# ScalarE makes the low bits of every piece of the first weight, instead of every second piece

## The chip, the cores and the metric

The kernel runs on one core of a Trainium2 chip. The metric is device time in microseconds (us) for one execution. The core has TensorE (PE, matrix multiplies; its weight loads are listed as PEld), VectorE (DVE), ScalarE (ACT), GpSimd (POOL) and SyncE (SP), which here only issues DMAs. Each engine works through its own instructions in the order in which they were written out.

## The reference, cut to what matters

Two parts follow each other: a landmark (Nystrom) attention over q, k and v of shape 8 x 8 x 576 x 64, and, on its output x of 8 x 576 x 512, a Fourier mixing, a normalisation and a two-layer MLP with weights of 512 x 2048 and 2048 x 512.

```python
A, Bm, C = sm(q, k_lm), sm(q_lm, k_lm), sm(q_lm, k)      # 32 landmarks: means of 18 rows
Z = Bm.T / (norm1(Bm) * norminf(Bm) + 1e-06)
for _ in range(6):
    Z = 2 * Z - Z @ Bm @ Z                               # Newton steps to the inverse
x = (A @ Z @ C @ v)                                      # then heads side by side
u = x + real(fft2(x))
un = (u - mean(u)) / sqrt(var(u) + 1e-06)
out = u + relu(un @ w_ch1) @ w_ch2
```

Both weights come as float64. q, k and v are float32.

## The kernel before, in words

One generator per job (`attention`, `weights`, `mlp`) gives out instructions. A planner in `run` keeps a clock of its own (`now`) from rough costs, and resumes the first of them that is due: attention has priority 1, weights 2, the MLP 3. So each instruction's place follows from what the planner thinks that the earlier ones cost. TensorE's order is written out exactly as the planner gave it. While nothing is due, and the MLP's second layer has not begun, the planner puts filler matmuls (`acc<-idle,ones`, 128x256) on TensorE, whose result nobody reads. On the other engines, a scheduler places the instructions by the same order, with extra order edges that the class `Timed` adds. All VectorE, ScalarE and GpSimd instructions go through `Timed` (line L138 in the profile), all matmuls through `mm` (L243), transposes through `tr` (L252), the fillers that are asked for by number through `warm` (L247).

The part around the change is `weights`. A weight is 16 pieces of 128 x 512 numbers, each piece a DMA of 512 KB of raw float64 words. There are 32 pieces: 0 to 15 of the first weight, 16 to 31 of the second. Each goes through:

1. `prepare`: one ScalarE Prelu of the words' upper halves makes sign and magnitude (`row<-w`, or `row<-big` where the raw words lie in a `big` buffer). It runs up to four pieces ahead.
2. The three low bits that float32 still takes from the words' lower halves. For even pieces VectorE shifts the lower half right by 29 (TENSOR_SCALAR `w<-w` 128x512 int32). For odd pieces ScalarE scales the top byte of the lower half and rounds it (ACTIVATE `w<-w` 128x512 int32 from uint8).
3. The joining: VectorE ors the shifted magnitude and the low bits (SCALAR_TENSOR_TENSOR `w<-row,w`). I call it the decode of the piece.
4. `squares`: four small matmuls of the piece on itself (`acc<-w` 128x128) that add up to a Gram matrix, two pieces behind the decode. Ahead of the last of a weight stand 24 fillers.
5. After the last piece of a weight, `scale` takes the diagonal (`wd`, `wm`), sums it by a matmul (`h<-wm,ones` for the first weight), takes a power on GpSimd (`wp_r<-wp_e`) and writes the weight's scale `wsc`.
6. `halve`: the split of a piece into a high and a low float16 half, ScalarE for the high (`w<-w,wsc`), VectorE for the low (SCALAR_TENSOR_TENSOR `w<-w,wsc`). The first weight's splits begin once its scale is known, two with each decode of the second weight (`PACE = 2`). The high half of piece i is written over the float32 room of piece i-2, so ScalarE's split of i waits until VectorE's split of i-2 has read it.

Beside it runs batch 0 of the attention: row sums of k and q, scores, softmax, six Newton steps (`RE`, `E`), a transform of the folded scores (`big<-at` after the matmuls `at<-t,mid` and `at<-t1t,row`), the product with v (`R`), its bound (`wm`), the factors `Wt` and `Wx`, their transform (`mid<-at` 128x262), and then in `mix` and `norm`: row tiles `u`, their statistics (`bn`), the normalised rows (TENSOR_SCALAR `row<-u,mv,r`, "the normalised tiles" below), their transposes on TensorE (`at<-ident,row`) and the split of those into `unT`.

The MLP works on two row tiles at a time (a chunk). A pair of the first weight's split pieces gives one `h` (24 matmuls `h<-unT,w` of 128x256), which ScalarE (Relu, the high half) and VectorE (the low half) evict. `h` has two PSUM buffers. Eight `h` make up a chunk. The second layer (`acc<-w,h` or `acc<-w,mid` 128x512) begins once the second weight has its scale and its first splits.

Of the kernel before, what the change touches and what calls it, by code (L numbers as in the profile page):

```python
# [20 lines left out]
NF = DF // P  # L21
# [12 lines left out]
AHEAD, PREP, EARLY = 1, 4, 2  # L34
# [124 lines left out]
class Kernel:  # L159
# [119 lines left out]
    def weights(self):  # L279
        nc = self.nc  # L280
        V, A = self.V, self.A
        whole = self.whole
        slots = [[t[:, OFF + 512 * i : OFF + 512 * i + 512] for i in range(NF)] for t in whole]
        upper = [[t.bitcast(BF16).rearrange("p (m x) -> p m x", x=2)[:, :, 1] for t in ss] for ss in slots]
        hl = [[t[:, 512 * i : 512 * i + 512].bitcast(F16).rearrange("p (y m) -> p y m", y=2) for i in range(NF)] for t in whole]
        self.w1s = [t.rearrange("p y (c f) -> p y c f", c=KT) for t in hl[0]]
        self.w2s = hl[1]
        sc = self.cp.tile([P, 3], F32, name="wsc")
        pieces = [(w, f) for w in range(2) for f in range(NF)]
        mags = []  # L290

        def prepare(i):


            mag = self.row(512)
            top = self.wraw[i].rearrange("p (m x) -> p m x", x=2)[:, :, 1].bitcast(F32)
            A.late = self.raw_there[i] if i < 2 * NF - PREP else 0.0
            A.activation(mag, top, AF.Prelu, scale=2.0**-112, alpha=-(2.0**32))
            mags.append(mag)

        def squares(i):

            w, f = pieces[i]
            if i == NF - 1:
                self.warm(24)
            for c in range(KT):
                x = upper[w][f][:, P * c : P * c + P]
                self.mm(self.gram[:, P * w : P * w + P], x, x, i == 0 and c == 0, f == NF - 1 and c == KT - 1)

        es = []  # L310

        def scale(w):

            dg, a2 = self.small(P, "wd"), self.small(1, "wm2")
            V.tensor_tensor(dg, self.gram[:, P * w : P * w + P], self.ident, ALU.mult)
            V.tensor_reduce(a2, dg, AX.X, ALU.add)
            if w:
                self.sum(1, 0, 2)
            yield self.till(a2, banks=1) if w else max(0.0, self.there[a2.name] - self.now)
            ps = self.psum() if w else self.ps_h.tile([P, 512], F32, name="h")  # L320
            self.mm(ps[:, 0:1], self.ones, a2)
            if w == 0:
                self.warm(8)
            self.scaled = True
            e, r = self.small(1, f"wp{w}_e"), self.small(1, f"wp{w}_r")
            V.tensor_scalar(e, ps[:, 0:1], 2.0**-120, 2.0**126, ALU.max, ALU.min)
            self.G.tensor_tensor(r, e, self.mhalf[:, 0:1], ALU.pow)
            if w:
                self.sum(1, 0, 3)
            V.tensor_scalar(r.bitcast(I32), r.bitcast(I32), 0x7F800000, None, ALU.bitwise_and)  # L330
            V.reciprocal(e, r)
            es.append(e)
            V.tensor_scalar(sc[:, w : w + 1], r, (2.0**12, 2.0**14)[w], None, ALU.mult)

        def halve():
            w, f = pieces[sum(self.split_w)]
            self.split(hl[w][f][:, 0], hl[w][f][:, 1], slots[w][f], sc[:, w : w + 1])
            self.split_w[w] = f + 1

        for i, (w, f) in enumerate(pieces):  # L340
            while len(mags) < min(2 * NF, i + 1 + PREP):
                j = len(mags)
                while len(self.wraw) < min(2 * NF, j + 1 + AHEAD):
                    self.raw()
                if self.raw_there[j] > self.now:
                    if j > i:
                        break
                    yield self.raw_there[j] - self.now
                    continue
                prepare(j)  # L350
            low = self.wraw[i].rearrange("p (m x) -> p m x", x=2)[:, :, 0]
            x, dst = mags[i].bitcast(I32), slots[w][f].bitcast(I32)
            (A if i % 2 else V).late = self.raw_there[i] if i < 2 * NF - PREP else 0.0
            if i % 2 == 0:
                V.tensor_scalar(dst, low, 29, None, ALU.logical_shift_right)
            else:
                byte = self.wraw[i].bitcast(mybir.dt.uint8).rearrange("p (m x) -> p m x", x=8)[:, :, 3]
                A.activation(dst, byte, AF.Copy, scale=2.0**-5, bias=-0.484375)
            V.scalar_tensor_tensor(dst, x, 3, dst, ALU.logical_shift_left, ALU.bitwise_or)
            if i > 1 and not NF <= i < NF + 2:  # L360
                squares(i - 2)
            self.decoded = i + 1
            if self.decoded == 2 * NF:
                self.load(1)
            yield max(0.0, max(self.V.free, self.G.free) - self.now - WT)
            if i == NF - 1:
                squares(NF - 2)
                yield 0.0
                squares(NF - 1)
                yield from scale(0)  # L370
            for _ in range(PACE if es else 0):
                if self.split_w[0] < NF:
                    halve()
                    yield max(0.0, max(self.V.free, self.G.free) - self.now - WT)
        squares(2 * NF - 2)
        self.lm1 = self.sums(None)
        self.sum(1, 0, 0)
        yield 0.0
        squares(2 * NF - 1)
        self.sum(1, 0, 1)  # L380
        self.magnitude(1, 0)
        yield from scale(1)
        V.tensor_scalar(sc[:, 2:3], es[0], 2.0**-25, es[1], ALU.mult, ALU.mult)
        self.inv2 = sc[:, 2:3]
        while sum(self.split_w) < 2 * NF:
            halve()
            yield max(0.0, max(self.V.free, self.A.free) - self.now - WT)
# [55 lines left out]
    def sum(self, b, e, i):  # L443

        loads, lm = (self.loads[1], self.lm1[0]) if b == 1 and e == 0 else (self.live, self.lm)
        V = self.V
        V.late = self.now if b == 2 else 0.0
        x, o = divmod(i, 2)
        if x == 0:
            part, kf = lm[:, 1, e, 32 * o : 32 * o + 32], loads[e][0][:, S * o : S * o + S]  # L450
            first = V.tensor_reduce(part, kf.rearrange("p (m t) -> p m t", t=18), AX.X, ALU.add)
        else:
            lv = lm[:, 0, e].rearrange("p (x o m) -> p x o m", o=2, m=8)
            qv = loads[e][1][:, 0 : 16 * SEG].rearrange("p (x o t) -> p x o t", o=2, t=2 * SEG)
            first = V.tensor_reduce(lv[:, :, o], qv[:, :, o, o : o + 144].rearrange("p x (m t) -> p x m t", t=18), AX.X, ALU.add)
        if b == 1:
            self.tc.keep_in_program_order(first)
# [664 lines left out]
```

## Time and profile before

| | before |
|---|---|
| median of 3 runs | 991.0 us (988.72 to 992.71) |
| profiled execution, its own time | 990.97 us |
| its span, first to last instruction | 989.2 us |
| what lies around the span | 1.8 us |
| PE busy | 959.0 us (97%), fillers included |
| DVE busy | 594.0 us (60%) |
| ACT busy | 319.7 us (32%) |
| mean granted TensorE clock | 0.989 of 2.4 GHz |

Busy times are sums over the whole span. A row's duration runs over into the next instruction of the same engine: two VectorE instructions of 0.68 us take 1.28 us, not 1.36, and three ScalarE instructions of 0.68 us take 1.83 us. So the text takes 0.60 us for such a VectorE instruction in a queue, and 0.57 to 0.60 us for a ScalarE one.

### The profile page before, as it was taken

To read this page: it belongs to the slowest core of one execution; us is meant where nothing else is said; L and a number is where in the kernel's file an instruction comes from. 1 tells how busy PE (TensorE), PEld (TensorE's weight loads), DVE (VectorE), ACT (ScalarE), POOL (GpSimd) and SP (SyncE) were. 2 spreads that over 40 slices of the span, in tenths; PEclk is the share of its full clock that TensorE was granted. 3 is DMA by queue.
4 is the path that set the end of the run, shared out by engine and by line. 5 is a ranking of instruction groups with operands and counts; after the bars stand their busy time and mean duration, and the time that the engine had idled before them with its cause. 6 is when DMAs were issued, how large, how long until landed. Compare 5 with 4: busy or idle time off the path is not lost.

```text
span 989.2 us, 20815 instructions
## 1 busy us (share of the span) xinstructions
PE 959.0 (97%) x8726; PEld 666.7 (67%) x8726; DVE 594.0 (60%) x1609; ACT 319.7 (32%) x652; POOL 120.6 (12%) x124
## 2 busy tenths in 40 slices
PE   7878999999999999999999999999999999999998
PEld 5667756667666776677666776676666767666665
DVE  7889896895567735486467736784634835141111
ACT  5468743242224322143214322332213422020110
POOL 0000000022021301123011301150110401010000
PEclk7799999999999999999999999999999999999999
DMA  9844304235021511026112421145121301020000
GB/s 331 280 186 154 103 13 161 38 64 176 22 44 42 154 50 22 28 52 164 36 44 38 110 99 43 23 62 172 22 34 33 51 3 42 22 34 23 1 22 22
DMA packets 97774, 74.66 MB, mean 75 GB/s; under 512 B 68112, under 2 KB 86544, under 8 KB 97552
## 3 DMA queue, kind: packets, MB, share of 16 engines
q1 hardware_dynamic: 97680, 73.34, 26.8%
q8 instruction: 68, 1.11, 0.5%
q14 instruction: 26, 0.21, 0.1%
HBM read 48.02 MB, written 9.44 MB: 58 GB/s over the span
## 4 chain that ended last, share of the span: by engine, by line
PE 70%; DVE 1%; DMA 0%; ACT 0%; issue 0%; DVEq 0%
PE acc L243 30%; PE h L243 30%; PE at L243 10%; DMA out_dram<-u 0%; DVE u L138 0%; DVE h L138 0%; ACT h L138 0%; DVE w L138 0%; DVE row L138 0%; DVEq L138 0%
## 5 line engine op out<-in xcount | busy, mean ns | idle before, releaser
L243 PE MATMUL h<-unT,w 128*128 128x256 f16 x3456 | 408.4, 273 | 3.6 <-DVE w L138 2.9
L243 PEld LDWEIGHTS <-w 128*128 128x128 f16 (+1 forms) x3584 | 343.7, 98 | 76.8 <-DVE w L138 7.3
L243 PE MATMUL acc<-w,h 128*128 128x512 f16 x1632 | 380.9, 379 | 0.9 <-DVE w L138 0.9
L243 PEld LDWEIGHTS <-h 128*128 128x128 f16 x1632 | 157.2, 98 | 160.2 <-issue 3.7
L138 DVE SCALAR_TENSOR_TENSOR h<-h 128x512 f16<-128x512 f32 x136 | 93.6, 688 | 227.4 <-ACT h L138 227.3
L138 ACT ACTIVATE h<-h 128x512 f16<-128x512 f32 x136 | 81.1, 596 | 328.7 <-PE h L243 328.5
L138 POOL TENSOR_TENSOR r<-ve,mhalf 128x2 f32<-128x2 f32 (+1 forms) x20 | 13.7, 685 | 476.8 <-DVE ve L138 472.4
L138 POOL TENSOR_TENSOR mid<-mid 128x640 f16<-128x640 f32 (+2 forms) x36 | 49.6, 1388 | 165.6 <-ACT mid L138 128.8
L138 DVE TENSOR_REDUCE lm<-big 128x32 f32<-128x576 f32 x64 | 46.1, 742 | 3.0 <-DMA big<-k_dram 2.5
L243 PEld LDWEIGHTS <-big 128*128 128x128 f16 (+1 forms) x864 | 39.6, 102 | 8.0 <-issue 1.9
L243 PEld LDWEIGHTS <-mid 64*128 64x128 f16 (+1 forms) x624 | 30.2, 97 | 16.0 <-issue 9.5
L138 ACT CAST row<-row 128x512 f16<-128x512 f32 (+1 forms) x40 | 20.9, 554 | 61.7 <-DVE row L138 60.6
L138 POOL TENSOR_TENSOR row<-row 128x512 f16<-128x512 f32 (+1 forms) x33 | 35.4, 1088 | 38.0 <-ACT row L138 37.4
L138 DVE SCALAR_TENSOR_TENSOR u<-at,scw,w 128x128 f32<-128x128 f32 (+3 forms) x105 | 33.8, 389 | 7.2 <-PE at L243 5.2
L138 DVE SCALAR_TENSOR_TENSOR u<-acc,wsc,u 128x512 f32<-128x512 f32 x36 | 26.8, 748 | 11.1 <-PE acc L243 11.1
L243 PEld LDWEIGHTS at<-RE,E 128*128 128x128 f32 x192 | 26.9, 197 | 9.1 <-DVE RE L138 3.3
L243 PE MATMUL at<-RE,E 128*128 128x64 f32 (+1 forms) x192 | 29.4, 277 | 3.1 <-DVE RE L138 2.5
L138 DVE SCALAR_TENSOR_TENSOR w<-at,scw,w 128x262 f32<-128x262 f32 (+1 forms) x42 | 18.6, 486 | 22.5 <-ACT w L138 22.4
L138 DVE TENSOR_TENSOR E<-at,mask 128x256 f32<-128x256 f32 x48 | 20.1, 420 | 19.7 <-PE at L243 19.6
L243 PE MATMUL at<-mid,big 128*128 128x262 f16 (+1 forms) x288 | 31.2, 276 | 0.0
L138 DVE TENSOR_TENSOR mid<-mid 128x256 f32<-128x256 f32 (+2 forms) x52 | 30.8, 626 | 0.0
L138 DVE SCALAR_TENSOR_TENSOR big<-big,aq_r 128x1024 f16<-128x1024 f32 (+1 forms) x32 | 26.9, 870 | 3.5 <-ACT big L138 3.5
(184 smaller groups left out, 906.3 us busy)
## 6 DMA issues: line engine op xcount, KB each, us to landing
w<-w_dram SPq DMA_DIRECT2D x22, 512.0 KB, 6.7
big<-v_dram SPq DMA_DIRECT2D x16, 640.0 KB, 9.6
big<-q_dram SPq DMA_DIRECT2D x16, 584.0 KB, 5.9
big<-k_dram SPq DMA_DIRECT2D x16, 576.0 KB, 5.1
out_dram<-u SPq DMA_DIRECT2D x36, 256.0 KB, 2.0
big<-w_dram SPq DMA_DIRECT2D x10, 512.0 KB, 6.5
t<-t_dram SPq DMA_DIRECT2D x1, 1048.0 KB, 10.2
unT<-row SPq DMA_TRANSPOSE x64, 2.4
```

Source lines behind the costliest of these rows:

```text
L138: ins = call(out, *args, **kw)
L243: self.nc.tensor.matmul(out, a, b, start=start, stop=stop, skip_group_check=True)
```

## The change

For the first weight (`i < NF`, pieces 0 to 15) ScalarE makes the low bits of all pieces. For the second, even pieces stay with VectorE and odd ones with ScalarE.

```diff
             low = self.wraw[i].rearrange("p (m x) -> p m x", x=2)[:, :, 0]
             x, dst = mags[i].bitcast(I32), slots[w][f].bitcast(I32)
-            (A if i % 2 else V).late = self.raw_there[i] if i < 2 * NF - PREP else 0.0
-            if i % 2 == 0:
+            by_act = i % 2 or i < NF
+            (A if by_act else V).late = self.raw_there[i] if i < 2 * NF - PREP else 0.0
+            if not by_act:
                 V.tensor_scalar(dst, low, 29, None, ALU.logical_shift_right)
             else:
                 byte = self.wraw[i].bitcast(mybir.dt.uint8).rearrange("p (m x) -> p m x", x=8)[:, :, 3]
```

Eight VectorE instructions go and eight ScalarE instructions come. Because the planner's clock follows the cost of each engine, the places of many others change with them.

VectorE, where the first normalised tiles and their transposes stand. `wd`, `wm`, `wp_e`, `wp_r`, `wsc` are the steps of `scale`, `w_73<-w_73,wsc` a split of the first weight, `w_74<-row,w_74` a decode of the second, `row<-u,mv,r` the normalised tiles, `unT<-at,unT` the eviction of their transposes. Before:

```order
L138 TENSOR_TENSOR wd<-acc_109,ident 128x128
L138 TENSOR_TENSOR rt<-r_937 128x2
L138 TENSOR_REDUCE wm_1001<-wd 128x1
L138 SCALAR_TENSOR_TENSOR rt<-rt,ve 128x2
L138 SCALAR_TENSOR_TENSOR r_939<-rt,r_937 128x2
L138 TENSOR_SCALAR wp_e<-h 128x1
L138 TENSOR_SCALAR row<-u,mv,r_939 128x512 x2
L138 TENSOR_SCALAR wp_r<-wp_r 128x1
L138 RECIPROCAL wp_e<-wp_r 128x1
L138 TENSOR_SCALAR wsc<-wp_r 128x1
L138 SCALAR_TENSOR_TENSOR w_73<-w_73,wsc 128x512
L138 SCALAR_TENSOR_TENSOR unT<-at,unT 128x4x128 x2
```

The same place of the changed kernel:

```order
L138 TENSOR_TENSOR rt<-r_1013 128x2
L138 SCALAR_TENSOR_TENSOR w_74<-row,w_74 128x512
L138 SCALAR_TENSOR_TENSOR rt<-rt,ve 128x2
L138 SCALAR_TENSOR_TENSOR w_73<-w_73,wsc 128x512
L138 SCALAR_TENSOR_TENSOR r_1015<-rt,r_1013 128x2
L138 SCALAR_TENSOR_TENSOR w_74<-row,w_74 128x512
L138 TENSOR_SCALAR row<-u,mv,r_1015 128x512 x2
L138 SCALAR_TENSOR_TENSOR w_73<-w_73,wsc 128x512
L138 TENSOR_SCALAR w_74<-w_74 128x512
L138 SCALAR_TENSOR_TENSOR w_73<-w_73,wsc 128x512
L138 TENSOR_SCALAR w_74<-big 128x512
L138 SCALAR_TENSOR_TENSOR unT<-at,unT 128x4x128 x2
```

The steps of `scale` now stand far ahead of the normalised tiles; between `wsc` and `unT` there are eight splits, four decodes and three low-bit instructions of the second weight, where there was one split.

VectorE, a little earlier: where the scale is taken. `w_73<-row,w_73` is a decode of the first weight, `mid<-at,mid` the transform of `Wt`, `row<-at,scw,row` the first step of `mix`. Before, first, and then the changed kernel:

```order
L138 SCALAR_TENSOR_TENSOR mid<-at,mid 128x262 x4
L138 SCALAR_TENSOR_TENSOR w_73<-row,w_73 128x512
L138 TENSOR_SCALAR w_73<-w_74 128x512
L138 SCALAR_TENSOR_TENSOR w_73<-row,w_73 128x512
L138 SCALAR_TENSOR_TENSOR row<-at,scw,row 128x262 x2
L138 SCALAR_TENSOR_TENSOR w_73<-row,w_73 128x512
L138 TENSOR_SCALAR w_73<-w_74 128x512
L138 SCALAR_TENSOR_TENSOR u<-at,scw,row 128x256
```

```order
L138 SCALAR_TENSOR_TENSOR mid<-at,mid 128x262 x4
L138 SCALAR_TENSOR_TENSOR w_73<-row,w_73 128x512 x3
L138 TENSOR_TENSOR wd<-acc_109,ident 128x128
L138 TENSOR_REDUCE wm_915<-wd 128x1
L138 TENSOR_SCALAR w_74<-big 128x512
L138 TENSOR_SCALAR wp_e<-h 128x1
L138 TENSOR_SCALAR wp_r<-wp_r 128x1
L138 RECIPROCAL wp_e<-wp_r 128x1
L138 SCALAR_TENSOR_TENSOR row<-at,scw,row 128x262 x2
L138 TENSOR_SCALAR wsc<-wp_r 128x1
```

The last three decodes and the whole of `scale` moved ahead of `mix`; before they were spread through it.

TensorE, at the end of the Newton steps. `RE,E` 128x32 is the last step; `at<-t1t,row` ends a transform of the folded scores. Before, it stood behind the first of the two transforms; in the changed kernel it stands behind the second. First the rows before, then the changed ones:

```order
L243 MATMUL at<-t1t,row 128x320
L243 MATMUL at<-RE,E 128x32 x2
L243 LDWEIGHTS w_73
L243 MATMUL acc_109<-w_73 128x128
L243 LDWEIGHTS w_73
```

```order
L243 MATMUL at<-t1t,row 128x320
L243 LDWEIGHTS row
L243 MATMUL at<-t1t,row 128x320
L243 MATMUL at<-RE,E 128x32 x2
L243 LDWEIGHTS w_73
L243 MATMUL acc_109<-w_73 128x128
```

Between the second transform and the product `at<-R,Yd` there was nothing; now there are this last step, two pieces' squares and three fillers. The number of fillers in the whole program goes from 156 to 153.

## Rows read from the trace of the kernel before

**Rows 1.** The page: busy time of each engine, and the busy share in 40 equal slices of 24.7 us, in tenths (9 is 90% or more; PEclk is the granted clock in tenths).

```profile
PE 959.0 (97%) x8726; PEld 666.7 (67%) x8726; DVE 594.0 (60%) x1609; ACT 319.7 (32%) x652; POOL 120.6 (12%) x124
...
DVE  7889896895567735486467736784634835141111
ACT  5468743242224322143214322332213422020110
...
PEclk7799999999999999999999999999999999999999
```

**Rows 2.** Busy time of each engine by stretch: us from the span's start and length, then PE, PEld, DVE, ACT, POOL, the granted clock, the DMA share and GB/s.

```profile
0.00:71.00 71.00, 55.44 (x597) 42.50 (x598) 57.89 (x181) 37.18 (x79) 2.28 (x8) 0.86 0.80 277
71.00:86.00 15.00, 11.40 (x118) 8.80 (x117) 14.32 (x34) 13.58 (x28) 1.07 (x1) 1.00 0.30 105
86.00:116.00 30.00, 29.05 (x303) 25.54 (x301) 27.09 (x53) 22.27 (x40) 0.56 (x1) 1.00 0.51 159
...
400.00:980.00 580.00, 579.85 (x5087) 399.83 (x5085) 298.57 (x797) 149.24 (x304) 78.89 (x77) 1.00 0.20 49
```

**Rows 3.** What TensorE's matmuls waited for between 71 and 142 us: us in total, times, longest.

```profile
PE h L243 <- DVE w L138: 2.9, 4, 1.1
PE acc L243 <- DVE w L138: 1.3, 2, 0.9
PE h L243 <- DVE unT L138: 0.7, 1, 0.7
PE acc L243 <- ACT w L138: 0.5, 1, 0.5
```

**Rows 4.** Groups of VectorE and ScalarE instructions by form between 10 and 72 us: count, busy us, mean ns of one, idle time before. The first is the decode, the second the low bits on VectorE, the third the low bits on ScalarE.

```profile
L138 DVE SCALAR_TENSOR_TENSOR w<-row,w 128x512 int32<-128x512 int32 x16 | 10.9, 679 | 0.2
L138 DVE TENSOR_SCALAR w<-w 128x512 int32<-128x512 int32 x8 | 3.4, 420 | 0.0
L138 ACT ACTIVATE w<-w 128x512 int32<-128x512 uint8 x8 | 5.5, 685 | 0.0
```

**Rows 5.** The same between 71 and 89 us: VectorE's and ScalarE's splits.

```profile
L138 DVE SCALAR_TENSOR_TENSOR w<-w,wsc 128x512 f16<-128x512 f32 x9 | 6.7, 750 | 0.1
L138 ACT ACTIVATE w<-w,wsc 128x512 f16<-128x512 f32 x11 | 7.8, 718 | 0.7 <-DVE w L138 0.7
```

**Rows 6.** VectorE in order of time: start, duration (of all the instructions of the row), idle time before in brackets.

```profile
41.24 0.69 DVE L138 TENSOR_TENSOR mid<-mid 128x512 f16<-128x512 f32 x1
...
49.51 0.93 DVE L138 SCALAR_TENSOR_TENSOR big<-at,big 128x320 f16<-128x320 f32 x2 [1.85 <-ACT big L138]
50.34 0.28 DVE L138 TENSOR_REDUCE wm<-at 128x1 bf16<-128x128 f32 x1
...
54.41 0.48 DVE L138 SCALAR_TENSOR_TENSOR Wt<-E,wx_r,Wt 128x256 f16<-128x256 f32 x1
...
56.56 1.11 DVE L138 SCALAR_TENSOR_TENSOR mid<-at,mid 128x262 f16<-128x262 f32 x3 [0.41 <-ACT mid L138]
...
67.73 1.00 DVE L138 TENSOR_SCALAR row<-u,mv,r 128x512 f32<-128x512 f32 x2
...
69.06 0.13 DVE L138 TENSOR_SCALAR wsc<-wp_r 128x1 f32<-128x1 f32 x1
...
70.66 1.28 DVE L138 SCALAR_TENSOR_TENSOR unT<-at,unT 128x512 f16<-128x512 f32 x2
...
74.01 1.90 DVE L138 SCALAR_TENSOR_TENSOR u<-at,scw,row 128x256 f32<-128x256 f32 x6
```

**Rows 7.** TensorE in order of time, same columns.

```profile
42.07 1.36 PE L243 MATMUL at<-t,mid 128*128 128x160 f16 x12
...
44.28 1.06 PE L243 MATMUL at<-RE,E 128*128 128x32 f32 x4
45.15 0.61 PE L243 MATMUL acc<-w 128*128 128x128 bf16 x4
45.56 0.84 PE L243 MATMUL acc<-idle,ones 128*128 128x256 bf16 x3
...
48.85 0.67 PE L243 MATMUL at<-R,Yd 128*128 128x64 f32 x2
...
62.54 2.78 PE L247 MATMUL acc<-idle,ones 128*128 128x256 bf16 x24
...
68.42 1.09 PE L252 MATMUL at<-ident,row 128*128 128x128 f32 x8
69.34 1.52 PE L243 MATMUL at<-mid,big 128*128 128x262 f16 x12
...
71.99 0.71 PE L243 MATMUL h<-unT,w 128*128 128x256 f16 x5 [0.70 <-DVE unT L138]
...
88.06 2.78 PE L243 MATMUL h<-unT,w 128*128 128x256 f16 x24
```

**Rows 8.** One stretch by the columns of Rows 2: the slow-clock part of the transforms.

```profile
42.00:49.30 7.30, 7.30 (x54) 5.36 (x50) 4.27 (x11) 1.47 (x4) 0.00 (x0) 0.54 0.69 235
```

**Rows 9.** GpSimd's power in the first weight's scale, and VectorE's statistics of the first two tiles, in order of time on each engine.

```profile
67.89 0.87 POOL L138 TENSOR_TENSOR wp_r<-wp_e,mhalf 128x1 f32<-128x1 f32 x1 [1.10 <-DVE wp_e L138]
...
63.58 1.28 DVE L138 BATCH_NORM_STATS2 bn<-u 128x6 f32<-128x512 f32 x2
```

## The prediction

> **What bounds the kernel now.** The page first: TensorE is busy 97% of the span, VectorE 60%, ScalarE 32%, but the slices show two regimes. In the first four (to 99 us) VectorE is at 7 to 9 tenths and ScalarE at 4 to 7; later both fall away [rows 1]. The view by stretches says it sharper: from 400 to 980 us TensorE is busy 579.85 of 580 us, so whatever is late at 400 stays late to the end [rows 2]. Before that, 71 us pass until the first MLP matmul. TensorE's 55.4 busy us there are partly fillers, so its busy time proves nothing; from 71 to 86 us it has 3.6 idle us, from 86 to 116 only 0.95 [rows 2]. What it waits for there are VectorE's weight pieces and the first transposed tiles: 2.9 + 0.7 us for `h`, 1.3 + 0.5 for the second layer [rows 3]. So the kernel's time is: when does the first `h` begin, how well do the next four `h` run, and then TensorE's own work. Two streams must meet there: the tokens (attention of batch 0 to `unT`) and the first weight (decode, scale, split). Before, they meet almost exactly: the scale is out at 69.06, `unT` ends at 71.94 [rows 6], the first full run of `h` begins at 71.99 [rows 7].
>
> **The exchange itself.** Eight low-bit instructions leave VectorE, 0.420 us each, 0.34 in a queue: 2.7 us. Eight come to ScalarE, 0.685 each, 0.57 in a queue: 4.6 us [rows 4]. ScalarE is busy 37.2 of the first 71 us [rows 2], so its 34 idle us could take them in sum. The pieces' raw words and the DMAs are the same. All else is order, so I follow the first 83 us by the new order, with the old rows' durations.
>
> *To the end of the folded scores.* VectorE's last subtraction there ended at 41.9 [rows 6]. Three low-bit instructions are gone by then (-1.0 us). Against it, ScalarE now makes bits of the third piece ahead of the copies that feed the products with v (+0.57), and VectorE then waits for TensorE where it used to work. I take -0.2; ends -1.0 and +0.6.
>
> *To the bound `wm`.* This stretch runs at a granted clock of 0.54, that is nearly all at the lower level of 1.2 GHz, with TensorE busy all of it [rows 8]. The new order puts the last Newton step, two squares and three fillers between the second transform and `at<-R,Yd`: 0.87 + 2 x 0.41 + 0.64 = 2.3 us by the distances of the old rows' starts [rows 7]. The place between the two transforms has about as much as it had (+0.1). VectorE stands behind TensorE here either way: its old waits are the 1.85 us ahead of 49.51 and one before it [rows 6]. So `wm` moves from 50.34 to about 52.6 (+2.2). At full clock the new stretch would be about 2.5 us shorter; that is the low end (-0.3); the high end is +3.5.
>
> *To `Wt`.* The three extra decodes done by then came in VectorE's waits; between `wm` and `Wt` there are now two decodes instead of three and no low bits (-0.94), so 3.1 us instead of 4.07 (50.34 to 54.41 [rows 6]). `Wt` goes from 54.41 to 55.7.
>
> *To the scale.* The last `mid` ends at 58.9 instead of 57.67 [rows 6]. Now the last three decodes follow in a row (1.8 us, to 61.6 with the wait for ScalarE's bits). The 24 fillers, 2.78 us [rows 7], stand between the squares of the last two pieces; they used to run beside VectorE's work on `u`, now VectorE's next instruction is `wd`. It waits about 2.1 us, to 63.7. Then `wd`, `wm`, the `mix` matmuls that stand ahead of the sum (1.4 us [rows 7]), the power on GpSimd (0.87 us, 1.1 from `wp_e` to its use [rows 9]) and two VectorE instructions of `mix`: scale at 67.7 instead of 69.06, -1.4 us.
>
> *From the scale to the first tiles.* This is the term that decides. Before, the normalised tiles were ready at 68.73, ahead of the scale. Now VectorE has between the two, in this order and in one queue: four decodes (2.4), six splits (0.750 each [rows 5], 0.66 in a queue: 4.0), six `u` (1.8 [rows 6]), two statistics (1.2 [rows 9]), one low-bit instruction (0.34), small ones (0.6) and the tiles (0.95): 11.3 us, and 0.3 for the power in the norm. The tiles are ready at 67.7 + 11.6 = 79.3. From there to the end of `unT` it took 3.2 us (68.73 to 71.94); now two splits and two low-bit instructions stand in between, VectorE again has 3.2 us of work, and ScalarE's splits, each bound to VectorE's split two pieces back, leave its `unT` at about the same time. `unT` ends at 82.5; the first full run of `h` begins then, 10.5 us late.
>
> The Trainium skill says in "TensorE: Matmul & The Clock Gate", section "Architectural detail", that ScalarE and VectorE are strict first-in-first-out. The term above is what this makes of the new order; the rows above, where a ready instruction never passes a waiting one, agree.
>
> *What comes back.* The splits that were done early need not be waited for. From 71.99 to 88.06 four `h` were made, 16.1 us [rows 7]; their 96 matmuls at 0.109 us (24 in 2.62) are 10.5, with 1.6 of `mix` and squares 12.1. With eight pieces split at the start only the evictions hold TensorE up: ScalarE and VectorE reach them late, behind splits and statistics, and there are two PSUM buffers. I count 1.3 us: 13.5 us, so 2.6 come back, and 0.2 for squares that are done earlier. From 88 on TensorE was the bound; it stays so. The second weight's first split was waited for 0.5 + 0.4 us [rows 3]; the new order puts 30 matmuls of `h` behind its sum where there were 18, 1.3 us more cover, so these 0.9 go too. The third wait, 0.9 us for a piece at 127 us, I leave in.
>
> Sum: +10.5 at the first `h` (the terms up to there are in it), -2.6, -0.2, -0.9: +6.8 us. The profiled execution took 990.97 us, its span 989.2 with 1.8 around, and agrees with the median of 991.0. Predicted: **997.7 us**.
>
> **Bounds.** For the start of `h`: -3.5 (full clock and the early gain kept) to +2.5. For the evictions: 0 to 4 us instead of 1.3, since two of them may each meet a split and a statistic. For the waits behind: 0 to -1.8. Half of these together give 995 to 1001, the likeliest case's own range.
>
> **Rivals.**
> *A, the early splits pay for the late tiles (988.5 to 995, middle 992.5).* If the Newton end is not slow (-2.5), the evictions cost nothing (-1.3) and all waits of [rows 3] behind 88 us go (another -0.9), +6.8 becomes +2.1. For it: TensorE needs all splits sooner or later, and VectorE's total fell. Against: it can't begin a chunk without `unT`, and nothing but fillers stands in its queue meanwhile.
> *B, faster: VectorE's relief goes straight through.* VectorE is the busiest engine next to TensorE from 10 to 110 us, and 2.7 us leave it. If the tokens kept their old place, the first `h` would start up to 2.7 us earlier and the 5.4 us of [rows 3] would shrink by about half: 985.5. It decides if `unT` ends before about 75.5, the start at which the 3.7 us that come back (2.6 + 0.2 + 0.9) equal the delay. The order speaks against it: eight splits stand ahead.
> The Trainium skill's "Perfetto Trace Analysis", section "Optimizing Scalar/DVE Operations", says that with VectorE saturated, handing work to ScalarE may make sense, though a VectorE performance mode is faster; by that rule it would come out as B. The rows agree with both halves (0.420 against 0.685, VectorE fuller), but the rule is silent on the order that a planner makes of it.
> *C, ScalarE becomes the bound (1001 to 1006).* From 71 to 86 us it is busy 13.6 of 15 us [rows 2]. If its splits, Prelus and evictions queue ahead of `h` by one more instruction each (0.6 to 1 us for each of the first four to eight), 3 to 6 us come on top.
>
> **How the numbers follow.** About 0.5% (5 us) is what a measurement of this kernel can tell from no change. Forecast (995 to 1001) 0.47, A 0.33, B 0.08, C 0.12. Slower by over 0.5% means above 996: most of the forecast (0.42 of it) and C, 0.54; same 0.38 (A and the rest); faster 0.08. The range must leave out no more than 2 in 10: B below 988.5 and most of C above 1003.
>
> **What would show it.** Right: `wsc` at 66 to 69 us, but the tiles `row<-u,mv,r` behind it, near 79; the first long run of `h` at 80 to 84; no wait of `h` for VectorE's pieces, but some for `h`'s own buffers; TensorE some 7 us late at 400 us and free of waits from there; ScalarE's low bits 16 x 0.685, VectorE's none before 61 us. Wrong: `unT` before 76, or the transforms at full clock, or more than 3 idle TensorE us between its first and fourth `h`.

## The result, and the profile after

| | before | after |
|---|---|---|
| median | 991.4 us (988.72 to 992.71) | 998.3 us (997.68 to 999.13) |
| profiled execution, its own time | 990.97 us | 998.42 us |
| its span | 989.2 us | 996.6 us |
| mean granted TensorE clock | 0.989 | 0.984 |

The changed kernel takes 1.0084 times as long (95% interval 1.0066 to 1.0102). The medians, of four executions each, differ by 6.9 us (1.0070, which lies in that interval). The forecast was 997.7: near, and on its side. The steps in between did not all come out as written.

The page after: busy times and two of the slice rows, as in [rows 1].

```profile
PE 957.0 (96%) x8723; PEld 667.9 (67%) x8723; DVE 594.3 (60%) x1601; ACT 323.7 (32%) x660; POOL 118.9 (12%) x124
...
DVE  7879797786476745387367846683634835141111
ACT  6667653243224322043224322342212422111110
...
PEclk8888999999999999999999999999999999999999
```

VectorE has eight instructions less and ScalarE eight more. ScalarE's low bits between 10 and 72 us, one of them of the second weight, in the form of [rows 4]:

```profile
L138 ACT ACTIVATE w<-w 128x512 int32<-128x512 uint8 x17 | 11.1, 667 | 0.0
```

Over the whole span little of this is to be seen; the stretches tell more (columns of [rows 2]).

```profile
0.00:71.00 71.00, 49.53 (x575) 38.76 (x575) 55.24 (x166) 44.30 (x92) 1.26 (x7) 0.88 0.86 292
71.00:86.00 15.00, 8.17 (x75) 6.79 (x76) 14.29 (x36) 10.94 (x21) 1.14 (x1) 0.66 0.17 49
86.00:116.00 30.00, 29.17 (x308) 25.96 (x306) 24.55 (x50) 19.79 (x37) 1.07 (x1) 1.00 0.46 153
400.00:980.00 580.00, 579.85 (x5095) 400.80 (x5094) 298.85 (x796) 148.37 (x304) 78.66 (x77) 1.00 0.19 49
```

From 71 to 86 us TensorE is busy 8.17 us where it was 11.40. VectorE is as full there as before (14.29 of 15). From 400 us on nothing differs: the loss lies ahead of that, and nothing makes up for it behind. TensorE's waits from 71 to 142 us, in the form of [rows 3]:

```profile
PE at L252 <- DVE row L138: 9.7, 1, 9.7
PE at L243 <- DVE nrm L138: 1.4, 1, 1.4
PE h L243 <- DVE mid L138: 0.8, 1, 0.8
```

The waits of `h` and of the second layer for weight pieces are gone. One wait of 9.7 us, of the transposes for the normalised tiles (`row`), stands in their place. VectorE's own rows (as in [rows 6]) say why the tiles come late:

```profile
50.61 0.29 DVE L138 TENSOR_REDUCE wm<-at 128x1 bf16<-128x128 f32 x1 [0.62 <-PE at L243]
...
53.66 0.48 DVE L138 SCALAR_TENSOR_TENSOR Wt<-E,wx_r,Wt 128x256 f16<-128x256 f32 x1
...
57.05 0.43 DVE L138 SCALAR_TENSOR_TENSOR mid<-at,mid 128x262 f16<-128x262 f32 x1 [0.23 <-ACT mid L138]
...
62.83 0.29 DVE L138 TENSOR_TENSOR wd<-acc,ident 128x128 f32<-128x128 f32 x1 [2.31 <-PE acc L243]
...
66.14 0.14 DVE L138 TENSOR_SCALAR wsc<-wp_r 128x1 f32<-128x1 f32 x1
...
77.01 1.00 DVE L138 TENSOR_SCALAR row<-u,mv,r 128x512 f32<-128x512 f32 x2
...
79.93 1.29 DVE L138 SCALAR_TENSOR_TENSOR unT<-at,unT 128x512 f16<-128x512 f32 x2
```

The scale is out 2.9 us earlier than before (66.14 for 69.06), the tiles 9.3 us later (77.01 for 67.73). TensorE, as in [rows 7]:

```profile
49.54 0.41 PE L243 MATMUL at<-R,Yd 128*128 128x64 f32 x2 [0.76 <-ACT w L138]
...
53.63 2.96 PE L243 MATMUL at<-t,Wt 128*64 128x262 f16 x24 [1.59 <-ACT Wt L138]
...
62.57 1.52 PE L243 MATMUL at<-mid,big 128*128 128x262 f16 x12
...
77.69 1.94 PE L252 MATMUL at<-ident,row 128*128 128x128 f32 x8 [9.73 <-DVE row L138]
79.43 2.33 PE L243 MATMUL at<-mid,big 128*128 128x262 f16 x12
...
82.16 0.82 PE L243 MATMUL h<-unT,w 128*128 128x256 f16 x6
...
84.03 2.79 PE L243 MATMUL h<-unT,w 128*128 128x256 f16 x24
...
92.69 2.12 PE L243 MATMUL h<-unT,w 128*128 128x256 f16 x18 [0.83 <-DVE mid L138]
...
94.88 2.78 PE L243 MATMUL h<-unT,w 128*128 128x256 f16 x24
```

The first `h` comes at 82.16 instead of 71.99, 10.2 us late. The fourth, with the squares in between, is done after six matmuls of the run at 94.88, at 95.5 instead of 88.06: 7.5 us late, and the spans differ by 7.4.

### The profile page after: what moved, and what is told of

Its sections match the earlier page's. It is cut to its first block, busy times and chain, and to the rows that moved or that the text cites. A ratio compares the mean times of both kernels' runs of the same rounds, so it can differ in the third digit from the quotient of the medians.

```text
span 996.6 us, 20801 instructions
## 1 busy us (share of the span) xinstructions
PE 957.0 (96%) x8723; PEld 667.9 (67%) x8723; DVE 594.3 (60%) x1601; ACT 323.7 (32%) x660; POOL 118.9 (12%) x124
## 4 chain that ended last, share of the span: by engine, by line
PE 70%; DVE 1%; DMA 0%; ACT 0%; issue 0%; DVEq 0%
PE acc L243 30%; PE h L243 30%; PE at L243 10%; DMA out_dram<-u 0%; DVE u L138 0%; DVE h L138 0%; ACT h L138 0%; DVE w L138 0%; DVE row L138 0%; DVEq L138 0%
```

## The experiments

The theory: the eight moved instructions cost and gain nothing by themselves; the planner, whose clock follows them, takes the scale earlier and puts the splits ahead of the first tiles, and these late tiles are the time. The rivals: ScalarE's added work is the cost; VectorE's relief is a gain that something else hides; the lower clock behind TensorE's long wait is the cost. Beside the runs below, the kernel before took 989.2 to 989.4 us (medians); each ratio is against the executions of before on the same chip.

**The exchange without the new order, and the new order without the exchange.** In the first, ScalarE makes the bits but the planner is charged as if VectorE did, so TensorE's order is that of before. In the second VectorE still makes them and the planner is charged as if ScalarE did; TensorE's order is that of the changed kernel. The helper `charged` books an instruction's cost on the first engine it is given and issues it on the other.

```diff
+            if i % 2 == 0 and i < NF:
+                self.charged(V, A, V.fast, late, dst, low, lambda: nc.scalar.activation(dst, byte, AF.Copy, scale=2.0**-5, bias=-0.484375))
```

```diff
+            if i % 2 == 0 and i < NF:
+                self.charged(A, V, A.rate, late, dst, byte, lambda: nc.vector.tensor_scalar(dst, low, 29, None, ALU.logical_shift_right))
```

> The exchange alone: ScalarE makes the first weight's low bits, but the planner charges them to VectorE as before, so TensorE's order is that of the kernel before, and VectorE's differs by little more than the eight missing instructions. Theory (the order of splits and first tiles decides, the exchange is cheap): 988 to 992 us, first full run of h at 70 to 73 us. Rival (the dearer instructions on ScalarE are what costs): 995 to 999 us. Rival (VectorE's relief of 2.7 us goes straight through): 986 to 988.5 us.

> The new order alone: VectorE makes the even pieces' low bits as before, but the planner charges them to ScalarE as in the changed kernel, so TensorE's order is that of the changed kernel. Theory: 997 to 1001 us, tiles ready at 77 to 80 us and TensorE idle 9 to 12 us ahead of their transposes. Rival (the dearer instructions on ScalarE are what costs): 989 to 993 us.

The exchange alone: 990.5 us, ratio 1.0008 (0.9995 to 1.0021). The order alone: 996.7 us, ratio 1.0075 (1.0060 to 1.0091). So the order by itself is nearly the whole slowdown; the work that moved costs 0.08%, by the interval at most 0.21%. The order alone was a little faster than expected (997 to 1001 us, tiles ready from 77 us; they were ready at 76.4), and shows the same picture, VectorE first and then TensorE:

```profile
64.54 0.14 DVE L138 TENSOR_SCALAR wsc<-wp_r 128x1 f32<-128x1 f32 x1
...
75.41 0.99 DVE L138 TENSOR_SCALAR row<-u,mv,r 128x512 f32<-128x512 f32 x2
```

```profile
76.10 1.94 PE L252 MATMUL at<-ident,row 128*128 128x128 f32 x8 [9.73 <-DVE row L138]
```

**The tiles ahead of the splits.** The changed kernel, in which the first weight's splits wait until the first two tiles are given out:

```diff
+                while self.ntile < 2:
+                    yield 0.3
...
+            if w == 0 and f < 8:
+                self.tc.add_manual_dep(lo.ins, self.first_un, info, reason="order")
```

> The changed kernel, but the weights' job stops behind the first scale until the first two tiles are given out, and VectorE's first eight splits stand behind these tiles. ScalarE still makes all low bits of the first weight. Theory: the tiles are ready at about 72 us instead of 78, the first full run of h begins at about 74.5 instead of 82.2, and 991 to 995 us. Rival (the late Newton end and the wait for the Gram matrix are what costs): 996 to 999 us.

993.2 us, ratio 1.0040 (1.0025 to 1.0056): about half of the loss comes back. VectorE's scale and tiles, and TensorE's transposes and second layer:

```profile
65.04 0.14 DVE L138 TENSOR_SCALAR wsc<-wp_r 128x1 f32<-128x1 f32 x1
...
70.02 1.00 DVE L138 TENSOR_SCALAR row<-u,mv,r 128x512 f32<-128x512 f32 x2
```

```profile
70.71 1.94 PE L252 MATMUL at<-ident,row 128*128 128x128 f32 x8 [4.17 <-DVE row L138]
...
117.70 0.38 PE L243 MATMUL acc<-w,mid 128*128 128x512 f16 x1 [1.40 <-ACT w L138]
```

The tiles come 5.0 us behind the scale (65.04) instead of 10.9, and the wait ahead of the transposes shrinks from 9.73 to 4.17. It doesn't go; the scale still stands ahead of `mix` in this order, but no run moved it back, so that this is the reason is not shown. And with the weights' job held back, the second layer again waits for splits of the second weight, 1.40 + 0.41 us; that is as much as before (1.8 us by [rows 3]), where the changed kernel had no such wait.

**The clock behind the long wait.** Behind the 9.73 idle us TensorE's granted clock was 0.50 (the 1.2 GHz level) in the stretch from 76 to 81 us, and 0.99 from 81 to 86. The stretch, in the columns of [rows 2]:

```profile
76.00:81.00 5.00, 3.31 (x16) 2.80 (x17) 5.00 (x11) 3.02 (x5) 0.00 (x0) 0.50 0.08 30
```

So 85 fillers went into the gap:

```diff
+                if self.ntile == 1:
+                    self.warm(85)
```

> The changed kernel with 85 more fillers on TensorE in its idle 9.7 us ahead of the first transposes, so that its clock need not fall. 85 x 0.107 us are 9.1 us and end before the tiles are ready. If the fall to 1.2 GHz behind that gap costs what the rows say (transposes 1.94 instead of 1.09 us, the mix matmuls 2.33 instead of 1.52, the next ones 1.19 instead of 0.84): 996 to 997 us. If the evictions behind decide anyway: 998 to 998.5 us.

998.6 us, ratio 1.0089 (1.0071 to 1.0107): no gain. The transposes took 1.08 us, so the clock stayed up, but `h` then waited. TensorE, and then VectorE:

```profile
77.20 1.08 PE L252 MATMUL at<-ident,row 128*128 128x128 f32 x8 [0.45 <-DVE row L138]
...
82.27 0.71 PE L243 MATMUL h<-unT,w 128*128 128x256 f16 x5 [1.05 <-DVE unT L138]
```

```profile
79.43 1.59 DVE L138 SCALAR_TENSOR_TENSOR w<-w,wsc 128x512 f16<-128x512 f32 x2
80.94 1.28 DVE L138 SCALAR_TENSOR_TENSOR unT<-at,unT 128x512 f16<-128x512 f32 x2
```

Two splits that stand behind `unT` in the changed kernel stand ahead of it here: the scheduler had moved them when TensorE's order grew. So this run doesn't answer its question. The next holds them in their old places:

```diff
+            if w == 0 and 8 <= f < 10:
+                for ins, prev in zip(pair, self.turned):
+                    self.tc.add_manual_dep(ins.ins, prev, info, reason="order")
```

> The 85 fillers again, in TensorE's 9.73 idle us ahead of the first transposes, but with two splits held behind the first unT on VectorE and ScalarE, where the changed kernel has them; with the fillers alone they had slipped ahead of unT, 1.5 us of VectorE's queue. Up to unT the order of VectorE and ScalarE is now that of the changed kernel. If the fall of the clock costs time, it is the stretch from the end of unT (81.2 us) to the first h (82.16 us) in the changed kernel, at most 1.0 us: transposes 1.09 us at full clock, unT ends near 80.7, the first h follows it at once, and 997.0 to 997.7 us beside 998.3. Rival: nothing comes back, because VectorE's queue and not TensorE sets the time: 998 to 998.6 us.

995.9 us, ratio 1.0063 (1.0043 to 1.0083): by the ratios some 2 us less than the changed kernel, more than expected; the two intervals overlap, so the size of this gain is uncertain. VectorE's tiles, and TensorE:

```profile
75.02 0.99 DVE L138 TENSOR_SCALAR row<-u,mv,r 128x512 f32<-128x512 f32 x2
```

```profile
75.71 1.08 PE L252 MATMUL at<-ident,row 128*128 128x128 f32 x8 [0.45 <-DVE row L138]
...
79.26 0.71 PE L243 MATMUL h<-unT,w 128*128 128x256 f16 x5 [0.45 <-DVE unT L138]
...
81.15 2.79 PE L243 MATMUL h<-unT,w 128*128 128x256 f16 x24
```

From the tiles to the long run of `h` it takes 6.1 us (75.02 to 81.15) instead of 7.0 (77.01 to 84.03): the low clock cost 0.9 us there, within the bound of 1.0. With the two splits ahead of `unT` it had taken 7.6 (76.52 to 84.16). The other part is not the fillers' doing as far as the trace shows: in this profile the clock was also full ahead of them, from 50 to 62 us (0.86 in the changed kernel) and from 23 to 30 us, and the scale is out 2.0 us earlier (64.15). The stretch from 23 to 30 us, of the changed kernel and then of this run, in the columns of [rows 2]:

```profile
23.00:30.00 7.00, 6.67 (x155) 5.48 (x156) 4.99 (x11) 3.05 (x8) 0.00 (x0) 0.76 1.08 351
```

```profile
23.00:30.00 7.00, 6.42 (x175) 5.51 (x175) 6.48 (x16) 3.28 (x9) 0.00 (x0) 1.00 1.08 351
```

The six executions of this run had a mean granted clock of 0.991 to 0.993, those of the kernel before on the same chip 0.990 to 0.995. So the remaining 0.63% is not due to the clock, and that is most of the loss.

**The fillers ahead of the Gram sum.** The prediction's wait of 2.1 us for them measured 2.31. Taken out, in the changed kernel and in the tiles-first kernel:

```diff
-            if i == NF - 1:
-                self.warm(24)
```

> The changed kernel without the 24 fillers (2.78 us) that stand ahead of the last squares of the first weight. VectorE waited 2.31 us there for the Gram sum. If this wait is part of the delay, as the prediction has it: that wait under 0.4 us, the scale near 64.0 us instead of 66.14, the tiles near 74.9 instead of 77.01, and 996 to 996.7 us beside 998.3. Rival: nothing is won, because TensorE without the fillers falls to the lower clock and mix takes longer, or ScalarE's splits end last: 997.5 to 998.7 us with the first long run of h still behind 81.5 us.

> The tiles ahead of the splits, and those 24 fillers gone as well. If the delay left in the tiles-first kernel (193 of a thousandth each: 993.2 against 989.2 to 989.4 us of before) is mainly this wait of 2.31 us and the low clock behind TensorE's 4.17 idle us: the tiles near 67.8 us instead of 70.02, TensorE's wait ahead of the transposes near 4.5 us, and 990.5 to 991.5 us. Rival: what is left comes from the order of TensorE behind 80 us (fewer h matmuls ahead of the second layer), then 992.7 to 993.7 us.

(The "193 of a thousandth each" is a slip of the pen: the delay meant is 993.2 less 989.3 us.) 997.2 us, ratio 1.0068 (1.0046 to 1.0090), and 992.1 us, ratio 1.0023 (1.0010 to 1.0037): 1.0 to 1.7 us less in each, by medians or ratios, where about 2 were expected; in both the interval overlaps that of the kernel with these fillers, so the gain is not clear of noise. The changed kernel without them, VectorE and then TensorE:

```profile
61.50 0.29 DVE L138 TENSOR_TENSOR wd<-acc,ident 128x128 f32<-128x128 f32 x1 [0.57 <-PE acc L243]
...
64.17 0.16 DVE L138 TENSOR_SCALAR wp_e<-h 128x1 f32<-128x1 f32 x1 [1.72 <-PE h L243]
...
66.06 0.14 DVE L138 TENSOR_SCALAR wsc<-wp_r 128x1 f32<-128x1 f32 x1
```

```profile
61.23 2.68 PE L243 MATMUL at<-mid,big 128*128 128x262 f16 x12
```

The wait did fall from 2.31 to 0.57 us. But without the fillers the `mix` matmuls ran 2.68 us instead of 1.52 (the row at 62.57 of the changed kernel), the sum behind them came late, VectorE waited 1.72 us for that (0.46 in the changed kernel), and the scale stands at 66.06 for 66.14. In this execution, the slowest of the six, everything was given back. In others the clock did not fall so far: with the tiles first and no fillers, the five executions with a mean granted clock of 0.990 or more took 990.27 to 992.17 us, the five with 0.986 took 992.71 to 993.93.

**VectorE's relief at one clock.** The profile of the exchange alone had full clock from 41 to 50 us, where before had 0.54 in nearly the same stretch [rows 8], so the two could not be set side by side. With 16 fillers more, in the 1.70 us that TensorE waited ahead of the fifth Newton step, in the kernel before and in the exchange with the old order:

```diff
+            if b == 0 and it == 4:
+                self.warm(16)
```

> The kernel before, with 16 more fillers on TensorE ahead of the fifth Newton step of batch 0, where it waited 1.70 us for VectorE at 39.6 us. In the profile of before the granted clock from 42 to 49.3 us was 0.54; in the profile of the exchange alone, with the same order of TensorE, it was full and everything behind it came about 2.7 us earlier. If this fall of the clock comes and goes between executions and carries through to the end, the fillers hold the clock up: granted clock 1.00 from 41 to 50 us, the scale near 66.5 us instead of 69.06, and 988 to 988.8 us with a smaller spread than the 987.8 to 992.9 of the kernel before. Rival: what is won there is lost again at the waits for the weight pieces, or the clock falls elsewhere: 989 to 990.5 with the same spread.

> The exchange alone in the old order, with the same 16 fillers, so that it stands beside the fillers alone at the same clock. VectorE has eight low-bit instructions less, 2.7 us. If this relief goes through (rival B of the prediction, in the old order) it is 1 to 2.7 us below the fillers alone: 985.5 to 987.5 us, and the waits of the h matmuls for VectorE's pieces between 71 and 142 us shrink from 2.9 us to under 2. If the relief is lost in VectorE's waits for TensorE ahead of 50 us, it is within 0.7 us of the fillers alone and the waits stay at 2.9 us.

989.3 us, ratio 0.9993 (0.9981 to 1.0005), and 990.4 us, ratio 1.0005 (0.9992 to 1.0019). Two stretches, of the fillers alone and then of the fillers with the exchange:

```profile
41.00:50.00 9.00, 8.35 (x93) 6.33 (x91) 8.63 (x25) 4.55 (x10) 0.00 (x0) 1.00 0.67 243
50.00:56.00 6.00, 4.25 (x39) 3.06 (x39) 4.77 (x14) 4.09 (x9) 0.00 (x0) 0.72 0.93 369
```

```profile
41.00:50.00 9.00, 7.81 (x87) 5.89 (x84) 7.78 (x23) 4.23 (x9) 0.00 (x0) 1.00 1.02 373
50.00:56.00 6.00, 4.28 (x41) 3.11 (x42) 4.93 (x15) 4.23 (x10) 0.00 (x0) 0.77 0.43 171
```

VectorE's `unT`, again of the fillers alone and then with the exchange:

```profile
69.04 1.28 DVE L138 SCALAR_TENSOR_TENSOR unT<-at,unT 128x512 f16<-128x512 f32 x2
```

```profile
69.20 1.28 DVE L138 SCALAR_TENSOR_TENSOR unT<-at,unT 128x512 f16<-128x512 f32 x2
```

With the clock full up to 50 us in both, the relief is gone by then: VectorE is busy 7.78 instead of 8.63 us from 41 to 50, and `unT` is 0.16 us later, not 2.7 earlier. What left VectorE came back as its waits for other engines. One of them, ahead of the last eviction of the folded scores, of the fillers alone and then with the exchange:

```profile
46.76 0.93 DVE L138 SCALAR_TENSOR_TENSOR big<-at,big 128x320 f16<-128x320 f32 x2 [0.17 <-ACT big L138]
```

```profile
47.20 0.93 DVE L138 SCALAR_TENSOR_TENSOR big<-at,big 128x320 f16<-128x320 f32 x2 [1.19 <-ACT big L138]
```

The waits of `h` for pieces are 2.9 us in 4 in both, as in [rows 3]. By the medians the exchange is even 1.1 us slower than the fillers alone, where with the relief lost at most 0.7 was expected; the intervals overlap, and a gain of 1 us or more is not seen. The fillers held the clock up at 41 to 50 us, and it fell behind them instead (0.72 and 0.77 from 50 to 56 us). The median didn't move, against the 988 to 988.8 that were expected; the range did (988.76 to 991.07 in 12 executions, against 987.75 to 993.05 in 23 of before).

## Why the prediction was right

**The main step held.** From the scale to the tiles I had summed 11.6 us from the old rows in the new order; it took 11.9 (66.14 to 78.01). From the tiles to the end of `unT` 3.2 us were forecast and 3.2 measured (78.01 to 81.22). The order alone gives 1.0075, and putting the tiles first takes half of that back. The Trainium skill's "TensorE: Matmul & The Clock Gate", section "Architectural detail", calls VectorE and ScalarE strictly first-in-first-out; the two splits that slipped ahead of `unT`, and took the long run of `h` from 6.1 to 7.6 us behind the tiles, agree with it.

**The end of the Newton steps was mis-sized.** The term was +2.2 us for `wm` (52.6) with a low end of -0.3 at full clock. Measured: 50.61, +0.3. The transforms ran at full clock in this execution, which the prediction had named as a sign of being wrong; the low end was the case. Against it the last folding subtraction ended at 42.9, not at 41.7. That was the clock, too: from 23 to 30 us it was 0.76 here, and 1.00 in the tiles-first kernel and in the last run with 85 fillers, which have the same order up to there and ended it at 41.8 and 41.6.

**What this won was lost again to the clock, twice, unforeseen.** `at<-t,Wt` took 2.96 us at a granted clock of 0.63 (53 to 56 us), where the exchange alone needed 1.83 at 1.00:

```profile
51.73 1.83 PE L243 MATMUL at<-t,Wt 128*64 128x262 f16 x24 [1.54 <-ACT Wt L138]
```

So `Wt` to the last `mid` took 3.8 us instead of 3.2. And behind the 9.73 idle us `mix` held the first `h` back to 82.16, 0.9 us behind `unT`. The scale came at 66.14 (forecast 67.7), the first `h` at 82.16 (82.5). The forecast was thus 2.0 us too late at `wm`, 1.6 at the scale and 0.3 at the first `h`. That it was met so nearly is partly luck: low clock that the sum did not have made up for the low clock that it had and that did not come.

**The Gram wait and the evictions were near.** 2.31 us against 2.1, and 0.83 against 1.3. Four `h` took 13.3 us (82.16 to 95.5) against 13.5.

**What comes back was over-counted.** I had 1.1 us more to come behind the fourth `h`. All three waits of the second layer for pieces went, 1.8 us by [rows 3]; but a new one came, 1.4 us of the next batch's attention for `nrm`, and from 142 to 400 us TensorE is busy 253.0 us instead of 253.9. Net nothing: 7.5 us late at the fourth `h`, 7.4 at the end.

**The rivals.** A was wrong although two of its conditions came true (full clock at the Newton end, waits gone): the first `h` was 10 us late all the same. B fell twice: the tiles lost their place, and in the old order the relief ends in waits (1.0008, and 1.0005 at one clock). The rule named beside it, of the Trainium skill's "Perfetto Trace Analysis", section "Optimizing Scalar/DVE Operations", gains nothing here: VectorE was the busier engine, but what left it became its waits for other engines (the row at 47.20). C fell: between 71 and 142 us none of TensorE's matmuls waited for ScalarE.

**What stays open.** With the tiles first and no Gram fillers 2.9 us are left by the medians (1.0023). Its trace shows the second layer waiting 1.4 us for a split of the second weight and the tiles still 5 us behind the scale; these were not taken apart further. Nor is it shown which part of the new order costs the half that the tiles-first kernel did not give back. No version was faster than the kernel before.

## What to carry to other kernels

Where a planner places instructions by estimated costs, a small exchange between engines is two changes, and they can be run apart: the work with the old charge, and the new charge with the old work. Read from the new order what now stands, in one queue, between a result that TensorE waits for and its inputs, and price it with the old rows; that told the time here within 1 us, though two errors cancelled on the way. And take a relief for a gain only if that engine had no waits just behind the work that leaves it.

## What the runs showed of the hardware that was not expected

TensorE's granted clock in the first 62 us differs between executions in which TensorE has the same order. From 23 to 30 us it was 0.76 in the changed kernel and 1.00 in two versions whose order is the same up to 48 us. From 53 to 56 us it was 1.00 in the exchange alone and 0.61 and 0.54 in the two kernels with 16 fillers more, though in the three microseconds before it TensorE was busy about as much (1.36, 1.25 and 1.27 of 3 us). A stretch at the lower level, 1.2 GHz, cost from 0.9 us (from the tiles to the long run of `h`) to 2.9 us: from the matmuls at 42.07 to `at<-R,Yd` at 48.85 [rows 7] it took 6.8 us, and 3.9 in the same kernel with 16 fillers more. Behind the gap that these filled, the clock fell in the next one in both profiles; and in the profiled execution without the Gram fillers, the matmuls behind the wait lost about what the shorter wait had won. What decides in which gap the clock falls was not settled.
